# Two blocks on a diagonal in the products, the merge and the solve of a chunked recurrence; state scaled by pairs of chunks

## The chip, the cores and the metric

The kernel runs on one core of one Trainium2 chip. The metric is the device time of one execution in microseconds (us). A run of the kernel before took 594.81 us in the median of three (593.76 to 598.04). In the profile PE is TensorE (its matmuls; PEld its weight loads), DVE is VectorE, ACT is ScalarE, POOL is GpSimd, and SP is the engine that issues the DMAs.

## The reference

For 4 sequences of 768 steps with 8 heads of 40 channels a state matrix S (40 x 40 a head) is carried along, and the output of a step is read before the step changes it:

```
y[t]  = r[t] . S
Sa    = S a[t]
S     = S * w[t] - outer(Sa, b[t]) + outer(v[t], k[t])
```

w lies in 0.85 to 0.95, the other inputs are normal numbers times 0.05 or 0.1. The eight heads of a step form a row of 320 channels, and this goes through a layer norm without bias, a matmul to 1280 channels, ReLU, a matmul back to 320, and a residual sum (called the MoE layer below).

## The kernel before, in words

The 768 steps are cut into 24 chunks of 32 steps (C = 32, D = 40, B = 16). The 32 pairs of sequence and head are split into two halves of 16; one half's 40 channels stand on partitions 0 to 39, the other's on 64 to 103 (`ROWS`). Within a chunk the recurrence is solved in matrix form. The steps for a chunk, each a function of the program:

- `prep` loads w and a (`wa`), k and b (`bk`). Two scans on VectorE (L338, L342) make the running decay `gE` and its counterpart `qE`; GpSimd multiplies a by `qE` into `x2s` (L350) and k, b by `gE` (L356). TensorE then forms all products of a with k and b (L366): one matmul for each of 16 pairs-of-heads, with the 104 rows of both halves at once. So that the halves don't mix, GpSimd clears the rows that would meet the wrong half (L348). VectorE applies sign and mask (L369), and DMAs carry the result to a DRAM tile `d_l` and back into `x2s`.
- `invert` takes the 32 x 32 triangular matrices of a slab (two chunks, after two slabs of one) and inverts their two 16 x 16 diagonal blocks on GpSimd (L416, L420; on VectorE for the first two chunks), and puts them into `d_h` in DRAM.
- `merge` loads them back into `hv` and makes the full inverse by two groups of matmuls (L441, L452), one 32 x 32 tile of the array for each of four quarters (`QUADS`), with ScalarE's copies `qm` (L443) and `tt` (L454) between them.
- `loads` brings v, r and v transposed; `xk` gets k and b transposed. GpSimd clears the `z` rows of `x5s` (L483).
- `chain` is the recurrence itself: L498 multiplies the state, L508 solves with `tt`, L512 copies u, L523 forms the update, and VectorE adds the old state (L532) and scales with the decay of the next chunk (L533). The next chunk's L498 waits for it.
- `post` makes the output of the chunk: transposes of u and of the state (L551, L563), the products of v and u with r (L578, again 104 rows with both halves), their masking on VectorE (L584) and the output matmuls (L595).
- `norm` and `moe` are the layer behind it for every two chunks: dense matmuls L766 (first layer) and L750 (second layer), with ScalarE's ReLU copy `hh` (L769) and VectorE's rest `hl` (L771) between them.

Matmuls are on fp32 and each is executed as two matmul instructions and two weight loads, so 16 matmuls in the code are 32 in the trace. Products in the MoE layer are fp32r with hi and lo parts.

The order of the instructions is written out ahead of time by `Plan.order`. Every step is a task with an engine, an estimated time, a due time counted in chunks, the tiles it reads and writes, and the PSUM banks that it opens. The planner lays the tasks out engine by engine in simulated time: of what can start, the earliest due goes first. Of the eight PSUM banks four belong to group A (everything of the recurrence), two to the MoE's first layer and two to its second. The planner also limits how long small matmuls may run without dense ones between them, and counts matmul records against a price for fetching instructions. All DMAs are issued by SP in the planned order. On the chip each engine runs its tasks strictly in this order and waits on semaphores.

At the end the kernel looks over all w for values that it could not treat in this form, and would take a slow path, which these inputs do not need.

Of the kernel before, what the change touches and what calls it, by code (L numbers as in the profile page):

```python
# [11 lines left out]
F32 = mybir.dt.float32  # L12
# [4 lines left out]
ALU = mybir.AluOpType  # L17
# [165 lines left out]
def body(ctx, tc, ea, eb, vr, rd, vt, w1, w1x_in, w2, gl, fe, fd, out):  # L183
# [27 lines left out]
    start0, = ring(1, "start0", 16, 33)  # L211
# [11 lines left out]
    hv = ring(2, "hv", 8, 5 * B)  # L223
    qm, = ring(1, "qm", 8, C)
    tt = ring(2, "tt", 8, C)
# [22 lines left out]
    d_h = [dr.tile([32 * n, B, 3 * B], F32, name=f"d_h{s}") for s, (_, n) in enumerate(SLABS)]  # L248
# [10 lines left out]
    def dma(key, kb, rd, wr, to, of, parts=128, queue=2.0):  # L259
        P.add("SP", 0.35 + parts * 0.0006, lambda: sync.dma_start(out=to, in_=of), key, rd, wr, kb=kb, queue=queue)  # L260
# [3 lines left out]
    def consts():  # L264
# [27 lines left out]
        def f():  # L292
            V.memset(start0, 2.0 ** -33)
            V.memset(start0[:, :, 0:1], 1.0)
            V.memset(last, 0.0)
        op("DVE", 1.0, -95, (), ["start0", "last"], f)
        op("ACT", 0.3, -95, (), [("small", 0)], lambda: (A.memzero(small[0]["sd"]), A.sqrt(small[0]["sd"], small[0]["sd"])))
        for i in range(2):
            j = i + 1
            op("POOL", 0.8, -85 + i, (), two("hv", i, 4), lambda i=i: G.memset(hv[i], 0.0))  # L300

            def f(i=i):
                for q, qs in enumerate(QUADS):
                    up, lo = (ident[qs, 32 * q + B * x:32 * q + B * x + B].unsqueeze(1).broadcast_to([32, 8, B])
                              for x in range(2))
                    A.copy(out=hv[i][qs, :, 0:B], in_=lo)
                    A.copy(out=hv[i][qs, :, 4 * B:5 * B], in_=up)
                    if i == 0:
                        A.copy(out=qm[qs, :, 0:B], in_=lo)
            op("ACT", 2.6 if i == 0 else 1.8, -50 + i, ["ident"], two("hv", i, 4) + (["qm"] if i == 0 else []), f)  # L310
            op("POOL", 1.0, -40 + i, (), [("uT", i)] + two("vT", i), lambda i=i: G.memset(vu[i], 0.0))
            for t, x, us in ((x2, "x2", 1.4), (x5s, "x5s", 1.2), (xk, "xk", 1.4)):
                names = dict(
                    x2=two("S", i, 4) + two("v", i) + [("u", i)], x5s=two("r", i) + [("z", i)],
# [9 lines left out]
    def prep(c):  # L324
# [4 lines left out]
        W, K, A = two("wa", i), two("bk", k), two("x2a", x) + two("x2k", x, 4)  # L329
# [4 lines left out]
        for hf in (1, 0):  # L334
# [3 lines left out]
        op("DVE", 1.35, kp, W + ["start0"], [("g", i)], lambda: nc.vector.tensor_tensor_scan(  # L338
            out=flat(g[R]), data0=t[R, 0:n], data1=flat(start0[R]), initial=0.0, op0=ALU.mult, op1=ALU.max), lock=True)
        op("DVE", 0.29, kp, [("g", i)], ["last"], lambda: nc.vector.reciprocal(  # L340
            out=last[R, :, C:33], in_=g[R, :, C:33]))
        op("DVE", 1.4, kp, W + ["last"], [("q", i)] + ([("go",)] if c == 0 else []), lambda: nc.vector.tensor_tensor_scan(  # L342
            out=flat(q[R])[:, ::-1], data0=t[R, n:0:-1], data1=flat(last[R])[:, ::-1], initial=0.0,
            op0=ALU.mult, op1=ALU.max), lock=True)
        eng, e, us = ("DVE", nc.vector, 1.0) if c < EARLY else ("POOL", nc.gpsimd, 1.8)
        for hf, rs in enumerate(ROWS):
            if c >= XS:
                op("POOL", 0.6, kp - 0.3, (), [("x2k", x, 2 * hf), ("x2k", x, 2 * hf + 1)], lambda vs=slice(VROW[hf], VROW[hf] + C), hf=hf: nc.gpsimd.memset(  # L348
                    x2s[x][vs, hf, 0:512], 0.0))
# [3 lines left out]
            op("ACT", 0.25, kp + (1.0 if c < 2 else 0.0), [("g", i)], [("x2p", x, hf)], lambda hf=hf, rs=rs: nc.scalar.copy(  # L353
                out=x2s[x][rs, hf, 512:528], in_=g[rs, :, C:33].rearrange("p h o -> p (h o)")))
# [4 lines left out]
        b = Bank("A")  # L359

        def f(b=b):
            pg = bank[b.at].rearrange("p (f n t) -> p f n t", f=2, t=C)
            for h in range(8):
                for bb in range(2):
                    p = 8 * bb + h
                    mm(pg[64 * bb:64 * bb + 64, :, h], lhsT=tb[R, 64 * p:64 * p + 64], rhs=x2s[x][R, :, 32 * p:32 * p + 32],  # L366
                       start=True, stop=True)
        op("PE", 1.08, kp + 0.3, K + A, [b], f, opens=[b], room=[("gk", i)], recs=32.8)
        op("DVE", 0.72, kp + 0.3, [b, "sign"], [("gk", i)] + ([("first",)] if c == 1 else []), lambda b=b: nc.vector.tensor_tensor(  # L369
            out=gk[i].rearrange("p (n t) -> p n t", t=C), in0=bank[b.at].rearrange("p (n t) -> p n t", t=C),  # L370
            in1=sign.unsqueeze(1).broadcast_to([128, 16, C]), op=ALU.mult))
        for bb in range(2):
            m = 32 * j + 16 * bb
            dma(kp + 0.3, 140, [("gk", i)], [("d_l", s, 2 * j + bb)], d_l[s][m:m + 16].rearrange("m a t -> a m t"),
                gk[i][64 * bb + C:64 * bb + 64].rearrange("a (m t) -> a m t", t=C), 512)
        for hf in range(2):
            for bb in range(2):
                dma(kp + 0.4 + (1.0 if c < 2 else 0.0), 33, [("gk", i)], [("x2k", x, 2 * hf + bb)],
                    x2s[x][VROW[hf]:VROW[hf] + C, hf, 256 * bb:256 * bb + 256],
                    gk[i][64 * bb:64 * bb + C, 256 * hf:256 * hf + 256])  # L380
# [15 lines left out]
    def invert(s):  # L396
# [6 lines left out]
        eng, e, us = ("DVE", nc.vector, 0.54) if c0 < 2 else ("POOL", nc.gpsimd, 0.9)  # L403
# [3 lines left out]
        dma(k0, 262, L, Y, y[:, 0:1024], d_l[s].rearrange("m a t -> m (a t)"))  # L407
# [16 lines left out]
        dma(k0 + 0.4, 131, Y, [("d_h", s, 0)], d_h[s][:, :, B:3 * B], rows[:, 0:B])  # L424
# [544 lines left out]
```

## Time and profile before

| what | before |
|---|---|
| median of the runs | 594.81 us (593.76 to 598.04) |
| the profiled execution | 596.33 us, of which the span from first to last instruction is 594.6 |
| granted TensorE clock, mean | 0.961 |
| busy: TensorE, VectorE, ScalarE, GpSimd | 87%, 69%, 52%, 46% |
| matmul instructions | 14902, with as many weight loads |
| moved by DMA | 58.58 MB in 119670 packets |

The page gives busy time, the chain of work that ended last, and groups of instructions; a group's row has line, engine, operation, tiles out<-in, shapes, count, then busy time and mean duration, then idle time of the engine before them with what ended it. The rows of a stretch of time have TensorE's, its weight loads', VectorE's, ScalarE's and GpSimd's busy time with counts, the granted clock, the DMA share and the rate. Rows of the order of time have start, duration, engine, line, tiles and count.

### The profile page before, as it was taken

The numbers are of one execution on the slowest core, as the hardware profiler recorded it, in microseconds if no ns is written. First come the engines' busy times: TensorE is split into PE (matmuls) and PEld (weight loads), VectorE is DVE, ScalarE is ACT, GpSimd is POOL, SyncE is SP. The second block draws the span as 40 slices with busy tenths as digits, with TensorE's granted clock in tenths as the row PEclk, the third lists the DMA queues.
The fourth block names the chain that finished last, engine by engine and source line by source line (L and its number), as shares of the span: only waits on it lengthen the run. The fifth ranks groups of instructions, "written<-read, shape, count | busy, mean of one in ns | idle before, by whom it ended". The sixth has DMA issues, their size and how long they took to land.

```text
span 594.6 us, 33557 instructions
## 1 busy us (share of the span) xinstructions
PE 517.6 (87%) x14902; PEld 469.0 (79%) x14902; DVE 410.9 (69%) x907; ACT 311.2 (52%) x790; POOL 276.2 (46%) x510
## 2 busy tenths in 40 slices
PE   2527988799989899999899899899799899799996
PEld 2426766788879799888898798789799798688995
DVE  6699787787766667766676577686587667578622
ACT  8535768475465274373555365546456544555321
POOL 9425273374665572854824644674736706200000
PEclk9999779899989799998999899999999999899999
DMA  5465554425532435334243334434343344432000
GB/s 155 113 175 154 164 163 131 112 66 127 114 81 76 105 72 112 89 96 109 70 99 95 87 76 100 106 78 117 63 100 107 83 106 104 105 98 80 3 23 26
DMA packets 119670, 58.58 MB, mean 99 GB/s; under 512 B 100576, under 2 KB 106720, under 8 KB 119520
## 3 DMA queue, kind: packets, MB, share of 16 engines
q1 hardware_dynamic: 119520, 56.39, 38.6%
q8 instruction: 118, 1.93, 1.3%
q14 instruction: 32, 0.26, 0.1%
HBM read 44.56 MB, written 9.44 MB: 91 GB/s over the span
## 4 chain that ended last, share of the span: by engine, by line
PE 66%; POOL 8%; DVE 7%; issue 7%; ACT 5%; DMA 5%; SPq 1%; POOLq 0%; ACTq 0%; DVEq 0%
PE bank L750 17%; PE bank L766 16%; PE bank L366 4%; PE bank L578 4%; POOL ytmp L416 4%; POOL yv L420 4%; PE bank L595 2%; PE bank L498 2%; PE bank L508 2%; PE bank L441 2%; PE bank L452 2%; PE bank L563 2%; PE bank L473 2%; PE bank L523 2%; PE bank L551 2%
## 5 line engine op out<-in xcount | busy, mean ns | idle before, releaser
L750 PE MATMUL bank<-w,hh 128*128 128x320 f32 x480 | 119.9, 335 | 0.6 <-issue 0.6
L766 PE MATMUL bank<-xh,w 128*128 128x256 f32 x480 | 109.7, 290 | 4.4 <-issue 2.5
L769 ACT ACTIVATE hh<-bank 128x256 fp32r<-128x256 f32 x120 | 45.9, 384 | 116.4 <-PE bank L766 115.3
L771 DVE SCALAR_TENSOR_TENSOR hl<-bank,hh 128x256 fp32r<-128x256 f32 x120 | 49.9, 421 | 70.0 <-ACT hh L769 68.6
L766 PEld LDWEIGHTS bank<-xh,w 128*128 128x128 f32 x480 | 84.3, 193 | 4.4 <-issue 2.6
L750 PEld LDWEIGHTS bank<-w,hh 128*128 128x128 f32 x480 | 79.4, 195 | 7.6 <-issue 3.8
L356 POOL TENSOR_TENSOR bk<-bk,gE 104x1024 f32<-104x1024 f32 x22 | 48.9, 2222 | 65.7 <-issue 26.6
L750 PE MATMUL bank<-w,hl 128*128 128x320 f32 x240 | 76.2, 317 | 1.6 <-issue 1.6
L766 PE MATMUL bank<-xl,w 128*128 128x256 f32 x240 | 68.7, 286 | 0.2 <-issue 0.2
L350 POOL TENSOR_TENSOR x2s<-wa,qE 40x512 f32<-40x512 f32 x44 | 54.7, 1244 | 20.3 <-DVE qE L342 17.8
L420 POOL TENSOR_TENSOR yv<-yv,ytmp 64x28 f32<-64x28 f32 (+6 forms) x154 | 54.5, 354 | 12.1
L416 POOL TENSOR_TENSOR ytmp<-yv 64x28 f32<-64x28 f32 (+6 forms) x154 | 54.5, 354 | 11.4
L483 POOL MEMSET x5s<- 64x512 f32 x48 | 25.1, 522 | 71.6 <-PE bank L595 69.7
L532 DVE TENSOR_TENSOR bank<-bank,x 40x320 f32<-40x320 f32 x88 | 44.0, 500 | 11.2 <-PE bank L523 5.7
L478 ACT COPY xk<-bank 64x320 f32<-64x320 f32 x96 | 40.2, 419 | 21.7 <-PE bank L473 19.8
L584 DVE TENSOR_TENSOR x5s<-bank,mask 64x256 f32<-64x256 f32 x96 | 40.5, 422 | 15.4 <-PE bank L578 11.6
L766 PEld LDWEIGHTS bank<-xl,w 128*128 128x128 f32 x240 | 46.5, 194 | 3.1 <-issue 1.7
L750 PEld LDWEIGHTS bank<-w,hl 128*128 128x128 f32 x240 | 46.8, 195 | 1.4 <-issue 1.4
L512 ACT COPY x<-bank 32x320 f32<-32x320 f32 x96 | 40.1, 417 | 14.1 <-PE bank L508 12.8
L533 DVE TENSOR_TENSOR x<-bank,x2s 40x320 f32<-40x320 f32 x92 | 44.9, 489 | 3.1
L566 ACT COPY xk<-bank 40x320 f32<-40x320 f32 x96 | 40.2, 418 | 4.7 <-PE bank L563 3.0
L338 DVE TENSOR_TENSOR_SCAN gE<-wa,start 104x528 f32<-104x528 f32 x24 | 31.3, 1305 | 8.5 <-DMA wa<-in_ea_dram 4.8
(130 smaller groups left out, 1071.2 us busy)
## 6 DMA issues: line engine op xcount, KB each, us to landing
wa<-in_ea_dram SPq DMA_DIRECT2D x48, 162.7 KB
bk<-in_eb_dram SPq DMA_DIRECT2D x48, 160.0 KB
wa<-in_ea_dram SPq DMA_DIRECT2D x24, 165.0 KB
x<-in_vt_dram SPq DMA_DIRECT2D x48, 80.0 KB
x5s<-in_rd_dram SPq DMA_DIRECT2D x48, 80.0 KB
vu<-in_vr_dram SPq DMA_DIRECT2D x48, 80.0 KB
out_dram<-ot SPq DMA_DIRECT2D x24, 160.0 KB
r<-in_w_dram SPq DMA_DIRECT2D x10, 320.0 KB
```

Of the source, the lines that this page charges most:

```text
L350: op(eng, 0.75 * us, kp, W + [("q", i)], [("x2a", x, hf)], lambda hf=hf, rs=rs: e.tensor_tensor(out=x2s[x][rs, hf, 0:512].rearrange("p (h ...
L356: op(eng, 1.25 * us, kp, [("g", i)], K, lambda: e.tensor_tensor(out=kb, in0=kb, in1=g[R, :, 0:C].unsqueeze(2).broadcast_to([104, 16, 2, C] ...
L416: e.tensor_tensor(out=tv, in0=yb[:, :, j + 1:, j:j + 1].broadcast_to(S), in1=yb[:, :, j:j + 1, 0:j].broadcast_to(S), op=ALU.mult)
L420: e.tensor_tensor(out=v, in0=v, in1=tv, op=ALU.add)
L478: op("ACT", 0.45, c - 1.2 + 0.1 * bb, [bs[hf]], [X[hf]], lambda b=bs[hf], zs=zs, hf=hf, bb=bb: nc.scalar.copy(out=xk[i][zs, hf, 8 * bb:8 * ...
L532: nc.vector.tensor_tensor(out=p, in0=p, in1=x2[i][rs, hf, ps], op=ALU.add)
L533: nc.vector.tensor_tensor(out=x2[o][rs, hf, ps], in0=p, in1=x2s[xo][rs, hf, 512 + 8 * bb:520 + 8 * bb].unsqueeze(2).broadcast_to([D, 8, D] ...
L584: op("DVE", 0.46, k + 0.5, [b, "mask"], [("z", i)], lambda b=b, zs=zs, ps=ps, hf=hf, bb=bb: nc.vector.tensor_tensor(out=x5s[i][zs, hf, 8 * ...
L750: mm(bank_of(po[u])[:, 0:CH], lhsT=l[:, us], rhs=ws[f"w2_{f // 2}"][:, f % 2, x], start=f == 0 and n == 0, stop=f == 9 and n == 2)
L766: mm(ph, lhsT=l, rhs=r, start=n == 0, stop=n == 7)
L769: yield "ACT", 0.39, [phs[f]], [("hh", f % 2)], lambda f=f: nc.scalar.activation(out=hht[f % 2], in_=bank_of(phs[f])[:, 0:256], func=AF.Re ...
L771: yield "DVE", 0.46, [phs[f], ("hh", f % 2)], [("hl", f % 2)], lambda f=f: nc.vector.scalar_tensor_tensor(out=hlt[f % 2], in0=bank_of(phs[ ...
```

## The change: what it does

- **Products.** The matmuls of a with k and b (L366) and of r with v and u (L578) are done for each half by itself, on its 40 rows: 32 matmuls in the code in place of 16, each 32 wide in place of 64. The two halves go to two banks, and together with the two output halves (partitions 0 to 63 and 64 to 127) they make four tiles of the array. Nothing has to be cleared for this, so GpSimd's fills L348 and L483 are left out. VectorE takes each bank by itself (two operations in place of L369).
- **Merge and solve.** Two quarters are put on the diagonal of one 64 x 64 block. `hv` has nine blocks of 16 columns, `qm` four, `tt` 64 columns; the matmuls of L441, L452 and L508 become half as many, on 64 rows. ScalarE's copy into `tt` becomes four, one for each quarter, since each has its own columns. `d_h` is stored by rows, and the loads into `hv` differ between even and odd quarters (for the even ones three pieces of 16 columns, apart).
- **v with room for u.** The host lays v transposed with 32 zeros behind each 32 values. The load fills the whole tile `vu` in long runs, the half for u too.
- **State by pairs.** The decay is counted over two chunks. `qE` is scanned first, from a start table with 1 at the end for even chunks, and from the even chunk's last column for odd ones; `gE` follows from its reciprocal. The state is then only added after an even chunk, and added and scaled after an odd one. After chunk 0 ScalarE copies it.
- **The planner's costs** are changed along with it: the task times of the new groups, a time for each DMA's issue, and sizes of some DMAs.

```diff
+        h = c % 2
+        if h:
+            op("DVE", 0.15, kp, [("q", 0)], [("start", 1)], lambda: nc.vector.tensor_copy(
+                out=start[1][R, :, C:33], in_=qE[0][R, :, 0:1]))
...
         for hf, rs in enumerate(ROWS):
-            if c >= XS:
-                op("POOL", 0.6, kp - 0.3, (), [("x2k", x, 2 * hf), ("x2k", x, 2 * hf + 1)], ... memset(
-                    x2s[x][vs, hf, 0:512], 0.0))
...
-                    mm(pg[64 * bb:64 * bb + 64, :, h], lhsT=tb[R, 64 * p:64 * p + 64], rhs=x2s[x][R, :, 32 * p:32 * p + 32],
-                       start=True, stop=True)
+                    for hf, rs in enumerate(ROWS):
+                        p = 8 * bb + h
+                        mm(bank[bs[hf].at][64 * bb:64 * bb + 64, C * h:C * h + C], lhsT=tb[rs, 64 * p:64 * p + 64],
+                           rhs=x2s[x][rs, hf, 32 * p:32 * p + 32], start=True, stop=True)
...
-                for qs in QUADS:
-                    mm(po[qs, h], lhsT=qm[qs, h], rhs=right[qs, h], start=True, stop=True)
-        op("ACT", 0.4, km, [b], [("tt", i)], lambda b=b: nc.scalar.copy(
-            out=tt[i], in_=bank[b.at][:, 0:8 * C].rearrange("p (h t) -> p h t", h=8)))
+                for ps in halves:
+                    mm(po[ps, h], lhsT=qm[ps, h], rhs=blocks(hv[i], 4)[ps, h], start=True, stop=True)
+        for q, qs in enumerate(QUADS):
+            op("ACT", 0.39, km, [b], [("tt", i, q)], lambda b=b, qs=qs, q=q: nc.scalar.copy(
+                out=tt[i][qs, :, C * (q % 2):C * (q % 2) + C],
+                in_=bank[b.at][qs, 0:8 * C].rearrange("p (h t) -> p h t", h=8)))
...
-            dma(c - 0.6, 82, (), [("vT", i, hf)], vu[i][rs, :, 0], vr[c, hf])
+            dma(c - 0.6, 110, (), [("vT", i, hf), ("uT", i)], vu[i][rs], vr[c, hf])
...
-            op("POOL", 0.6, c - 0.7, (), [("z", i)], lambda zs=zs, hf=hf: nc.gpsimd.memset(x5s[i][zs, hf], 0.0))
...
-                for qs in QUADS:
-                    mm(bank[b.at][qs, h * D:h * D + D], lhsT=tt[i][qs, h], rhs=hn[i][qs, h], start=True, stop=True)
+                for ps in (slice(0, 64), slice(64, 128)):
+                    mm(bank[b.at][ps, h * D:h * D + D], lhsT=tt[i][ps, h], rhs=hn[i][ps, h], start=True, stop=True)
...
+                        if c == 0:
+                            nc.scalar.copy(out=to, in_=p)
+                        elif c % 2 == 0:
+                            nc.vector.tensor_tensor(out=to, in0=p, in1=old, op=ALU.add)
+                        else:
+                            nc.vector.tensor_tensor(out=p, in0=p, in1=old, op=ALU.add)
+                            nc.vector.tensor_tensor(out=to, in0=p, in1=x2s[x][rs, hf, ...], op=ALU.mult)
...
-                    mm(pz[64 * bb:64 * bb + 64, :, h], lhsT=vu[i][R, p].rearrange("p x t -> p (x t)"), rhs=x5s[i][R, :, p],
-                       start=True, stop=True)
+                    for hf, rs in enumerate(ROWS):
+                        p = 8 * bb + h
+                        mm(bank[bs[hf].at][64 * bb:64 * bb + 64, C * h:C * h + C], lhsT=vu[i][rs, p].rearrange("p x t -> p (x t)"),
+                           rhs=x5s[i][rs, hf, p], start=True, stop=True)
```

165 lines of the change are left out of this document (84 added, 81 removed).

## The prediction

> **What bounds the kernel now.** I read the page first, for the engines and the chain of waits, then the table by stages, then the groups, then the order of instructions on TensorE.
>
> ```profile
> span 594.6 us, 33557 instructions
> ...
> PE 517.6 (87%) x14902; PEld 469.0 (79%) x14902; DVE 410.9 (69%) x907; ACT 311.2 (52%) x790; POOL 276.2 (46%) x510
> ...
> PE 66%; POOL 8%; DVE 7%; issue 7%; ACT 5%; DMA 5%; SPq 1%; POOLq 0%; ACTq 0%; DVEq 0%
> ```
>
> ```profile
> core 0: us, PE busy (x) PEld busy (x) DVE busy (x) ACT busy (x) POOL busy (x), PEclk, DMA share, GB/s
> 0.00:120.00 120.00, 77.97 (x2067) 64.87 (x2071) 94.45 (x205) 73.57 (x178) 59.33 (x106) 0.91 0.55 144
> 120.00:560.00 440.00, 410.89 (x12638) 375.82 (x12627) 306.67 (x677) 231.36 (x596) 216.87 (x405) 0.97 0.39 92
> ```
>
> Two thirds of the chain is TensorE. The stages tell where. In the first 120 us TensorE is busy for 78 us and VectorE for 94: start-up and weights set the pace. From 120 to 560 us TensorE is busy 410.9 of 440 us, ScalarE only 231 and GpSimd 217. So I treat the stretch after 120 us as bound by TensorE and price the change by what TensorE's groups of matmuls cost there. A busy time is no price, since matmuls overlap; the price of a group is the time from its start to the start of the group behind it, where the two stand without a gap. These are pieces of TensorE's order of time (start, duration, line, tiles, count):
>
> ```profile
> 265.96 0.72 PE L441 MATMUL bank<-hv 32*32 32x16 f32 x64
> 266.61 1.15 PE L578 MATMUL bank<-x5s,vu 104*64 104x64 f32 x32
> 267.70 0.75 PE L452 MATMUL bank<-hv,qm 32*32 32x32 f32 x64
> 268.38 1.15 PE L366 MATMUL bank<-x2s,bk 104*64 104x64 f32 x32
> 269.46 0.56 PE L750 MATMUL bank<-w,hh 128*128 128x320 f32 x2
> ...
> 296.23 0.48 PE L473 MATMUL bank<-ident,bk 40*64 40x40 f32 x16
> 296.64 1.15 PE L366 MATMUL bank<-x2s,bk 104*64 104x64 f32 x32
> 297.72 0.79 PE L508 MATMUL bank<-hn,tt 32*32 32x40 f32 x64
> 298.44 0.55 PE L733 MATMUL bank<-ident,xn 128*128 128x128 f32 x3
> ...
> 301.12 0.83 PE L523 MATMUL bank<-x,xk 64*40 64x40 f32 x64
> 301.88 0.64 PE L551 MATMUL bank<-ident,x 32*40 32x32 f32 x32
> 302.45 0.41 PE L750 MATMUL bank<-w,hh 128*128 128x320 f32 x1
> ```
>
> Start to start: the two merge groups L441 0.65 and L452 0.68 us; the products L578 1.09 and L366 1.08; the solve L508 0.72; L523 0.76; L551 0.57; L473 0.41. The two products are the dearest, with half as many matmuls as their neighbours. The reason to be read from the rows is what passes through a tile of the array, not the number of matmuls. L366 is 32 matmuls of 64 columns on two tiles (the two column halves): 16 rounds. L452 is 64 of 32 columns on four tiles, also 16 rounds, and costs 0.40 less. L551, 32 matmuls of 32 columns on two tiles, again 16 rounds, costs 0.57, not half of L452.
>
> How many of these groups lie in the bound stretch, from the groups after 120 us:
>
> ```profile
> L578 PE MATMUL bank<-x5s,vu 104*64 104x64 f32 x672 | 26.1, 234 | 0.6 <-ACT vu L554 0.3 <-issue 0.3
> L366 PE MATMUL bank<-x2s,bk 104*64 104x64 f32 x576 | 21.7, 230 | 2.4 <-issue 1.6 <-POOL bk L356 0.7
> ...
> L508 PE MATMUL bank<-hn,tt 32*32 32x40 f32 x1344 | 16.6, 199 | 0.5 <-ACT hn L501 0.5
> L452 PE MATMUL bank<-hv,qm 32*32 32x32 f32 x1280 | 15.8, 196 | 3.0 <-issue 2.1 <-ACT vu L554 0.9
> L441 PE MATMUL bank<-hv 32*32 32x16 f32 x1280 | 15.2, 181 | 3.7 <-issue 3.5
> ```
>
> That is 21 groups of L578 (672/32), 18 of L366, 21 of L508 and 20 each of L452 and L441.
>
> **The change, part by part.**
>
> *Products (L366, L578).* Each becomes 64 matmuls of 32 columns on 40 rows, on four tiles: two row halves by two column halves. Moving width and count are those of L452 (0.68); the placement on two row halves by two column halves is that of L523 (0.76, with 40 columns). I take 0.69, since the width is L452's; the bounds are L441's 0.65 and L523's 0.76. Saved 1.08 - 0.69 = 0.39, times 39 groups: 15.2 us (12.5 to 16.8).
>
> *Merge.* Two groups of 64 on four small tiles become two groups of 32 on two 64-row tiles, 32 columns wide. L551 has count, width and two tiles: 0.57. I take 0.58 each; the bounds are 0.57 and L508's 0.72. Saved 0.65 + 0.68 - 1.16 = 0.17, times 20: 3.4 us (from 3.8 down to a loss of 2.2).
>
> *Solve.* 32 matmuls on two tiles in place of 64 on four, still 40 wide. L551's 0.57 for 32 columns makes 0.71 for 40, against 0.72: halving the matmuls saves nothing, 0.2 us over 21 groups.
>
> Sum on TensorE after 120 us: 15.2 + 3.4 + 0.2 = 18.8 us.
>
> *Instruction stream.* Matmuls fall by 32 a chunk (two products +32 each, merge -64, solve -32), 768 of 14902, 5%. At most that share of the chain's 7% "issue" goes with them, 2 us; I count none.
>
> *ScalarE.* One copy of the merged matrix (L454) becomes four, one for each 32 rows. L512 copies 32 rows of a bank.
>
> ```profile
> L512 ACT COPY x<-bank 32x320 f32<-32x320 f32 x96 | 40.1, 417 | 14.1 <-PE bank L508 12.8
> ...
> L454 ACT COPY tt<-bank 128x256 f32<-128x256 f32 x24 | 8.9, 371 | 15.4 <-PE bank L452 15.2
> ```
>
> Four at no more than 0.417 against 0.371 is 1.3 us more a chunk, 26 us over 20 chunks, on an engine busy for 231 of 440. I cost it at nothing: the idle 209 us hide it. Without that cover it is the ACT rival below.
>
> *VectorE.* The state is scaled only after odd chunks, so half of L533 goes.
>
> ```profile
> L532 DVE TENSOR_TENSOR bank<-bank,x 40x320 f32<-40x320 f32 x80 | 40.0, 501 | 10.7 <-PE bank L523 5.2 <-ACT hh L769 3.6
> L533 DVE TENSOR_TENSOR x<-bank,x2s 40x320 f32<-40x320 f32 x80 | 39.1, 489 | 2.8
> L584 DVE TENSOR_TENSOR x5s<-bank,mask 64x256 f32<-64x256 f32 x84 | 35.5, 422 | 12.9 <-PE bank L578 10.4
> ```
>
> 40 of the 80 at 0.489 is 19.6 us less, and an even chunk's state is ready four operations (2 us) earlier. Against it the signed product is taken in two halves, at most two of L584's 0.42 where one was. With VectorE at 307 of 440 this moves the end by nothing, in my sum. In the first 120 us, where VectorE leads, chunks 0 and 2 lose four operations each (-3.9 us), the second start table adds one fill, priced as one such operation, and ScalarE's three extra copies stand in the first chunk's chain (+1.3): bounds -3.9 and +2, taken as 0.
>
> The two scans change places, and an odd chunk's scan starts from the even chunk's last column, through a copy of 16 columns; both stand in VectorE's order one after the other already, so the wait adds nothing. ScalarE's two small copies of the decay are made in odd chunks alone.
>
> *GpSimd.* All clearing of tiles before the products goes, four fills a chunk:
>
> ```profile
> L483 POOL MEMSET x5s<- 64x512 f32 x40 | 20.9, 523 | 71.3 <-PE bank L595 69.7
> L348 POOL MEMSET x2s<- 32x512 f32 x33 | 17.1, 520 | 23.0 <-PE bank L498 16.9 <-issue 4.4 <-POOL bk L356 0.5
> ```
>
> 38 us of work and 94 us of standing still ahead of it, with the scaling of k, b and the inversion queued behind. It was off the bound, so 0; the bound on the gain is in the second case below.
>
> *DMA and SP.* v is loaded with zeros beside it: twice the bytes, but 40 long runs instead of 640 short ones, so the issue on SP is shorter and not longer. It now also has to land before ScalarE writes u into the same tile; behind that copy stand ScalarE's ReLU copies. It can be issued as early as before, so 0. The even quarters of the merge's load go in pieces of a third; no row has that, from 0 to some tenths of SP time. The two-halves layout lets the copies of the first half leave before the second is done.
>
> **Sum.** The profiled execution took 596.3 us, span 594.6 and 1.7 around it; 596.3 - 18.8 = 577.5. The median of the runs is 1.5 below the profiled one, so the forecast is 594.8 - 18.8 = 576. Its own range, by the bounds above, the prologue's -3.9 to +2 and 2 us of issue: 568 to 587.
>
> **The cases.** A measurement here tells about 1%, 6 us, from no change.
>
> *TensorE's groups shrink as priced: 576, chance 0.58.* For it speak the unbroken rows above.
>
> *More than that: 562, chance 0.17.* TensorE stands idle for 29 of the 440 us, which belong to the others' lateness. If lighter VectorE, GpSimd and SP halve it, another 14 us go.
>
> *The products' gain is given back: 591, chance 0.12.* Each product now opens two of the four banks of its group where one did. If TensorE waits 0.39 at each for a second bank, only 3.6 of the 18.8 remain. The plan is made anew and can place them otherwise, hence the small chance.
>
> *ACT becomes late: 602, chance 0.08.* The four copies stand in ScalarE's queue ahead of the ReLU copies (L769) that the second layer's matmuls await. If each chunk's 1.3 us shows, 26 us over 20 chunks, the end is 594.8 - 18.8 + 26. It decides once the ReLU copy has less than 1.3 us to spare. Against it, ScalarE waits for TensorE before that copy, not the other way round:
>
> ```profile
> ACT hh L769 <- PE bank L766: 115.3, 88, 4.9
> ```
>
> *Weights bind: 613, chance 0.05.* L473 loads 64 columns of weights on two row halves for each of 16 matmuls in 0.41, 26 ns each. If that is the weights' price, a product of 64 such loads costs 1.64, 0.56 more than now: 39 times that is +22, less 3.6. Against it, L366 has 32 such loads in 1.08, and L473's price is also explained by its 40 moving columns in eight rounds. The Trainium skill, "TensorE: Matmul & The Clock Gate", section "LDWEIGHTS (loading the stationary operand)", gives columns/1.2 ns for a load, 53 ns for 64 columns, and Part 3 lets loads overlap matmuls only where the row group differs. By that rule I estimate 1.7 us for a product after the change, two row groups sharing 64 loads, about the price of this rival; but it asks 1.7 also of L366 with one row group, and the trace has 1.08, so the trace does not agree.
>
> Faster by over 1%: 0.58 + 0.17 = 0.75; within 1%: 0.12; slower: 0.13. The range 560 to 598 leaves out the two slow cases and the far end of the second.
>
> **What would show it.** After the change, start to start in unbroken rows: the products at 0.65 to 0.76 with 64 matmuls, the merge groups near 0.58, the solve at 0.71 in spite of its 32. GpSimd's fills of these tiles gone, about 20 us less of VectorE, 25 us more of ScalarE. TensorE's busy share in the middle should stay near 93%: if it falls and the groups did shrink, a wait took the gain, and its releaser (ACT's copies or a bank's reader) names the rival. If the products stay at 1.08, the reading by moving columns is wrong.

## The result, and the profile after

The changed kernel took 627.94 us in the median of four runs (623.41 to 631.58), the one before 595.55 us (593.76 to 598.04) beside it: a ratio of 1.054, with a 95% interval of 1.045 to 1.062. The change made the kernel slower by 5%; 576 us had been forecast, between 560 and 598. The profiled execution took 625.96 us. Its page has these lines for busy time, the granted clock in 40 slices, and the chain of waits:

```profile
span 624.2 us, 32083 instructions
...
PE 559.8 (90%) x14134; PEld 510.3 (82%) x14134; DVE 398.4 (64%) x896; ACT 336.4 (54%) x842; POOL 231.7 (37%) x424
...
PEclk9999557699579769999999999999999899999998
...
PE 77%; DMA 5%; DVE 5%; POOL 4%; issue 3%; ACT 3%; SPq 2%; ACTq 0%; POOLq 0%; DVEq 0%
```

All that was to become lighter did: VectorE 411 to 398 us, GpSimd 276 to 232, matmuls 14902 to 14134, "issue" on the chain (time in which an engine waits for nothing that the profile shows) from 7% to 3%. ScalarE rose by 25 us, as forecast. TensorE rose by 42 us of busy time, and its share of the chain from 66% to 77%. The table by stages, with the columns of the one shown of before:

```profile
0.00:120.00 120.00, 75.86 (x1593) 63.17 (x1595) 93.05 (x193) 67.84 (x160) 52.33 (x82) 0.80 0.55 142
120.00:560.00 440.00, 425.92 (x11510) 392.22 (x11508) 273.78 (x629) 244.11 (x619) 179.41 (x343) 0.94 0.40 96
```

From 120 to 560 us TensorE stands idle for 14 us; before it was 29. So no new wait took a gain. TensorE works more and gets through less: 11510 matmuls in this stretch against 12638, 9% fewer, where the whole kernel has 5% fewer. Two things are behind it. The first stands in TensorE's order of time (start, duration, line, tiles, count), in rows without a gap:

```profile
409.64 1.12 PE L523 MATMUL bank<-hn,tt 64*64 64x40 f32 x32
410.69 0.39 PE L785 MATMUL bank<-xh,w 128*128 128x256 f32 x1
...
422.47 1.14 PE L597 MATMUL bank<-x5s,vu 40*64 40x32 f32 x64
423.54 0.47 PE L583 MATMUL bank<-ident,x 40*40 40x40 f32 x16
...
425.95 1.12 PE L458 MATMUL bank<-hv 64*64 64x32 f32 x32
427.01 0.87 PE L614 MATMUL bank<-xk,x5s 128*32 128x40 f32 x64
427.81 1.12 PE L468 MATMUL bank<-hv,qm 64*64 64x32 f32 x32
428.86 0.47 PE L492 MATMUL bank<-ident,bk 40*64 40x40 f32 x16
...
431.28 1.14 PE L375 MATMUL bank<-x2s,bk 40*64 40x32 f32 x64
432.35 0.48 PE L492 MATMUL bank<-ident,bk 40*64 40x40 f32 x16
```

Start to start, the solve (L523) is at 1.05 us, the product of r (L597) and that of a (L375) at 1.07, the merge groups (L458, L468) at 1.06 and 1.05. The products did not become cheaper than their 1.08 and 1.09 by more than 0.02; the merge went from 0.65 + 0.68 to 2.11 and the solve from 0.72 to 1.05.

The second is the row PEclk: between about 60 and 240 us five of its slices stand at five or six, where the row of before never falls below seven:

```profile
PEclk9999779899989799998999899999999999899999
```

The stages where the time was lost are the same. VectorE's last operation on the MoE output of the fourth and of the seventh pair of chunks, and of the last one, starts before at

```profile
281.36 0.49 DVE L778 SCALAR_TENSOR_TENSOR ot<-bank,xt 128x320 f32<-128x320 f32 x1 [1.33 <-PE bank L750]
...
414.43 0.89 DVE L778 SCALAR_TENSOR_TENSOR ot<-bank,xt 128x320 f32<-128x320 f32 x2
...
588.20 0.93 DVE L778 SCALAR_TENSOR_TENSOR ot<-bank,xt 128x320 f32<-128x320 f32 x2 [0.51 <-PE bank L750]
```

and after at

```profile
315.97 0.89 DVE L797 SCALAR_TENSOR_TENSOR ot<-bank,xt 128x320 f32<-128x320 f32 x2
...
440.38 0.93 DVE L797 SCALAR_TENSOR_TENSOR ot<-bank,xt 128x320 f32<-128x320 f32 x2 [0.84 <-PE bank L769]
...
617.58 0.93 DVE L797 SCALAR_TENSOR_TENSOR ot<-bank,xt 128x320 f32<-128x320 f32 x2 [0.51 <-PE bank L769]
```

The changed kernel is 35 us late after four pairs, 26 after seven and 29 at the end: all of the loss arises in the first half, and none of it in the steady part. That doesn't fit groups that are dearer in every chunk, taken alone.

### The profile page after: what moved, and what is told of

Its sections match the earlier page's. It is cut to its first block, busy times and chain, and to the rows that moved or that the text cites. A ratio compares the mean times of both kernels' runs of the same rounds, so it can differ in the third digit from the quotient of the medians.

```text
span 624.2 us, 32083 instructions
## 1 busy us (share of the span) xinstructions
PE 559.8 (90%) x14134; PEld 510.3 (82%) x14134; DVE 398.4 (64%) x896; ACT 336.4 (54%) x842; POOL 231.7 (37%) x424
## 3 DMA queue, kind: packets, MB, share of 16 engines
q8 instruction: 112, 1.84, 1.3%
## 4 chain that ended last, share of the span: by engine, by line
PE 77%; DMA 5%; DVE 5%; POOL 4%; issue 3%; ACT 3%; SPq 2%; ACTq 0%; POOLq 0%; DVEq 0%
PE bank L769 18%; PE bank L785 18%; PE bank L375 4%; PE bank L523 4%; PE bank L468 4%; PE bank L597 4%; PE bank L458 4%; PE bank L614 3%; PE bank L538 3%; PE bank L583 3%; PE bank L492 3%; PE bank L513 2%; PE bank L571 2%; SPq L263 2%; PE bank L400 2%
## 5 line engine op out<-in xcount | busy, mean ns | idle before, releaser
L769 PE MATMUL bank<-w,hh 128*128 128x320 f32 x480 | 118.6, 332 | 1.2 <-issue 1.1
L358 POOL TENSOR_TENSOR x2s<-wa,qE 40x512 f32<-40x512 f32 x44 | 56.9, 1293 | 161.3 <-PE bank L513 76.9
L785 PE MATMUL bank<-xh,w 128*128 128x256 f32 x480 | 113.0, 298 | 0.0
L785 PEld LDWEIGHTS bank<-xh,w 128*128 128x128 f32 x480 | 86.6, 199 | 1.6
L432 POOL TENSOR_TENSOR yv<-yv,ytmp 64x28 f32<-64x28 f32 (+6 forms) x154 | 52.8, 343 | 12.1
L428 POOL TENSOR_TENSOR ytmp<-yv 64x28 f32<-64x28 f32 (+6 forms) x154 | 51.6, 335 | 11.3
L497 ACT COPY xk<-bank 64x320 f32<-64x320 f32 x96 | 40.1, 418 | 28.0 <-PE bank L492 26.3
L471 ACT COPY tt<-bank 32x256 f32<-32x256 f32 x96 | 34.9, 363 | 21.2 <-PE bank L468 20.1
L458 PE MATMUL bank<-hv 64*64 64x32 f32 x768 | 30.3, 229 | 15.7 <-DMA hv<-d_h 13.8
L375 PE MATMUL bank<-x2s,bk 40*64 40x32 f32 x1536 | 34.9, 241 | 10.3 <-ACT bank L657 3.3
L375 PEld LDWEIGHTS bank<-x2s,bk 40*64 40x64 f32 x1536 | 31.8, 159 | 13.5 <-ACT bank L657 3.5
```

The lines of the kernel that those rows point to most:

```text
L358: op(eng, 0.75 * us, kp, W + [("q", i)], [("x2a", x, hf)], lambda hf=hf, rs=rs: e.tensor_tensor(out=x2s[x][rs, hf, 0:512].rearrange("p (h ...
L375: mm(bank[bs[hf].at][64 * bb:64 * bb + 64, C * h:C * h + C], lhsT=tb[rs, 64 * p:64 * p + 64], rhs=x2s[x][rs, hf, 32 * p:32 * p + 32], star ...
L428: e.tensor_tensor(out=tv, in0=yb[:, :, j + 1:, j:j + 1].broadcast_to(S), in1=yb[:, :, j:j + 1, 0:j].broadcast_to(S), op=ALU.mult)
L432: e.tensor_tensor(out=v, in0=v, in1=tv, op=ALU.add)
L458: mm(po[ps, h], lhsT=hv[i][ps, h, 0:4 * B], rhs=blocks(hv[i], 5)[ps, h], start=True, stop=True)
L497: op("ACT", 0.45, c - 1.2 + 0.1 * bb, [bs[hf]], [X[hf]], lambda b=bs[hf], zs=zs, hf=hf, bb=bb: nc.scalar.copy(out=xk[i][zs, hf, 8 * bb:8 * ...
```

## The experiments

Each kernel is given with its median and its ratio to the kernel before on the same chip; the kernels ran on several chips, so that of two kernels the ratios compare better than the medians. The planner lays the order out anew for each, so a per cent between two kernels can come from the order alone. Unless said otherwise an edit is made to the changed kernel.

### Products or merge: one part undone at a time

The first run undoes the merge and the solve (four tiles of 32 x 32, as before) and keeps the split products:

```diff
-                for ps in halves:
-                    mm(po[ps, h], lhsT=hv[i][ps, h, 0:4 * B], rhs=blocks(hv[i], 5)[ps, h], start=True, stop=True)
-        op("PE", 0.56, km, two("hv", i, 4), [b], f, opens=[b], room=["qm"], recs=32.5)
+                for qs in QUADS:
+                    mm(po[qs, h], lhsT=hv[i][qs, h, 0:2 * B], rhs=hv[i][qs, h, 3 * B:4 * B], start=True, stop=True)
+        op("PE", 0.66, km, two("hv", i, 4), [b], f, opens=[b], room=["qm"], recs=64.5)
...
```

> The changed kernel with merge and solve undone (64 matmuls on four 32 x 32 tiles each, one copy into tt), all else changed. Theory W (loads of 64 weight columns set the price of a group): the two merge groups go from 0.95 and 1.04 back to 0.66 and 0.68 us and the solve from 1.06 to 0.72, 1.0 us a chunk, about 20 us: 608. Theory C (the half clock in the first 240 us took the time, and the longer groups are what brings it): half-clock time falls from 108 us to about 50 as before and the time to 580 or less. Theory P (the new products are to blame): no change, 628.

The second undoes the products (104 rows, with GpSimd's fills) and keeps merge and solve joined:

```diff
-                    for hf, rs in enumerate(ROWS):
-                        p = 8 * bb + h
-                        mm(bank[bs[hf].at][64 * bb:64 * bb + 64, C * h:C * h + C], lhsT=tb[rs, 64 * p:64 * p + 64],
-                           rhs=x2s[x][rs, hf, 32 * p:32 * p + 32], start=True, stop=True)
-        op("PE", 0.7, kp + 0.3, K + two("x2a", x), bs, f, opens=bs, room=two("gk", i), recs=64.8)
+                    p = 8 * bb + h
+                    mm(pg[64 * bb:64 * bb + 64, :, h], lhsT=tb[R, 64 * p:64 * p + 64], rhs=x2s[x][R, :, 32 * p:32 * p + 32],
+                       start=True, stop=True)
+        op("PE", 1.08, kp + 0.3, K + A, [b], f, opens=[b], room=two("gk", i), recs=32.8)
...
```

> The changed kernel with the products undone (32 matmuls over all 104 rows, GpSimd's fills are back), merge and solve joined. Theory W: a product costs 1.07 either way, so the time stays within 1% of 628, slightly up for the fills. Theory C with the products' fewer rows as what lowers the clock: half-clock time falls and the time goes to about 600. Theory P: back to 600 or less.

With the merge undone it took 648.74 us (1.090, interval 1.082 to 1.097); with the products undone 601.42 (1.010, 1.001 to 1.019). Undoing the part whose groups had become dearer made the kernel slower still, and undoing the part whose groups cost what they had cost won 26 us. So the prices of the groups are not all of it. The first kernel has 16438 matmuls, the second 12598.

### Both undone; and the planner told what the groups cost

Both undone, by the two edits above together (the solve's shown here), leaves the state by pairs, the room for u, the order of `d_h` and the planner's new DMA costs:

```diff
-                for ps in (slice(0, 64), slice(64, 128)):
-                    mm(bank[b.at][ps, h * D:h * D + D], lhsT=tt[i][ps, h], rhs=hn[i][ps, h], start=True, stop=True)
+                for qs in QUADS:
+                    mm(bank[b.at][qs, h * D:h * D + D], lhsT=tt[i][qs, h], rhs=hn[i][qs, h], start=True, stop=True)
...
```

> Products, merge and solve all as before; what stays of the change is the state by pairs, v with room for u, the layout of d_h and the planner's DMA prices. Theory W: 628 - 20 for merge and solve, and the shorter work of VectorE and SP helps: 575 to 590, under the kernel before. Theory C with the pairs' new start-up as its cause: still above 600, with the half clock in the first 240 us.

587.67 us (0.988, interval 0.980 to 0.996). What is left of the change is no loss, and perhaps a gain of 1%.

The other run keeps the changed kernel's work and corrects only the task times by which the planner orders it:

```diff
-        op("PE", 0.7, kp + 0.3, K + two("x2a", x), bs, f, opens=bs, room=two("gk", i), recs=64.8)
+        op("PE", 1.07, kp + 0.3, K + two("x2a", x), bs, f, opens=bs, room=two("gk", i), recs=64.8)
...
-        op("PE", 0.56, km, two("hv", i, 4), [b], f, opens=[b], room=["qm"], recs=32.5)
+        op("PE", 1.04, km, two("hv", i, 4), [b], f, opens=[b], room=["qm"], recs=32.5)
...
-        op("PE", 0.72, k, two("tt", i, 4) + [("hn", i)], [b], f, opens=[b], room=[("u", i)], recs=32)
+        op("PE", 1.06, k, two("tt", i, 4) + [("hn", i)], [b], f, opens=[b], room=[("u", i)], recs=32)
...
```

> The changed kernel with the planner's task times set to what the trace after shows (merge 1.04 and 1.05 where 0.56 stood, solve 1.06 for 0.72, products 1.07 for 0.70); the work is the same. Theory L (a plan made from wrong prices lays small matmuls too long in a row, the clock falls and TensorE waits): 10 to 30 us less, half-clock time down. Theory W alone: within 1% of 628.

608.06 us (1.023, interval 1.015 to 1.032): with the same instructions in another order 20 of the 32 us are gone. The granted clock of this kernel by slices, and its stages:

```profile
PEclk9999999689999999989999999999999999999998
```

```profile
0.00:120.00 120.00, 78.65 (x1584) 66.09 (x1586) 93.18 (x193) 69.23 (x163) 51.70 (x83) 0.95 0.55 143
120.00:280.00 160.00, 153.85 (x4283) 141.27 (x4279) 99.87 (x229) 93.51 (x236) 73.40 (x138) 0.98 0.40 98
280.00:560.00 280.00, 273.94 (x7747) 253.47 (x7747) 188.78 (x427) 162.86 (x413) 105.05 (x204) 1.00 0.41 102
```

The clock is 0.95 up to 120 us where it was 0.80 in the changed kernel. The time at half clock falls from 107.7 us, as the trace's clock records add up, to 26.3 in this execution. But it is the fastest of the four (604.18) and the only one at a mean clock of 0.98: the others took 606 to 612 us at 0.94, which makes some 70 to 75 us at half clock, as the records hold only full and half. So 45 us less at half clock went with 2 to 8 us in this kernel. The 20 us came with the order made from right task times; how much of them is the clock's, and why this order is granted more of it, the runs don't tell.

### What sets the price of a group

A kernel of its own issues groups of the same shapes between blocks of dense matmuls; it isn't the computation. Each shape is a list of tiles (first row, rows, first column), with W weight columns and N moving ones:

```diff
+            for h in range(8):
+                for t in range(2):
+                    mm(**args(DIAG, 64, 32, h, t))
+            dense(16)
...
```

> Not the computation: only fp32 matmul groups of eight rounds in the code (16 executed), each behind 16 dense matmuls, with weight columns, moving columns and tiles varied one at a time. Theory W (a round lasts as long as the loads of the weights' columns of one tile, whatever the tiles beside it and the moving columns): with 64 columns every group takes 0.88 to 0.93 us from its first to its last start, for 16, 32 and 64 moving columns, on two diagonal tiles, on two column halves or on four tiles; with 32 columns 0.55 to 0.60, also with 64 moving; with 40 columns about 0.62. Theory M (the prediction's, moving columns set it): with 64 weight columns 0.45 for 16 and 32 moving columns and 0.93 for 64; with 32 weight columns and 64 moving 0.93.

Rows of its order of time; behind the tiles stand rows*columns of the weights, then rows x moving columns:

```profile
30.42 0.73 PE L50 MATMUL bank<-x,w 32*32 32x16 f32 x64
38.18 0.75 PE L54 MATMUL bank<-x,w 32*32 32x32 f32 x64
45.96 1.11 PE L58 MATMUL bank<-x,w 64*64 64x16 f32 x32
54.11 1.12 PE L62 MATMUL bank<-x,w 64*64 64x32 f32 x32
62.26 1.15 PE L66 MATMUL bank<-x,w 64*64 64x64 f32 x32
70.44 0.69 PE L70 MATMUL bank<-x,w 64*32 64x32 f32 x32
78.17 1.08 PE L74 MATMUL bank<-x,w 64*32 64x64 f32 x32
86.29 1.14 PE L78 MATMUL bank<-x,w 40*64 40x32 f32 x64
94.46 1.10 PE L82 MATMUL bank<-x,w 40*32 40x64 f32 x64
102.59 0.83 PE L86 MATMUL bank<-x,w 40*40 40x40 f32 x64
110.45 1.12 PE L90 MATMUL bank<-x,w 104*64 104x32 f32 x32
```

Every group here is 16 rounds through each of its tiles. With 64 weight columns it lasts 1.11 to 1.15 us, whether 16, 32 or 64 columns move (L58, L62, L66). With 32 weight columns and 64 moving ones it is 1.08 and 1.10 as well (L74, L82). With 32 of each it is 0.69 and 0.75 (L70, L54), with 40 of each 0.83 (L86). So in these products the larger of the two numbers sets a round; neither "weights alone" nor "moving columns alone" holds. Two tiles or four makes no difference (L62 and L78). Joining two 32 x 32 blocks to one of 64 x 64 doubles the weight columns, and that is the whole price; splitting the products halved the moving columns from 64 to 32 and left 64 weight columns, and so the price stayed. The transposes against the identity are an exception: in the changed kernel's rows above L492, with 64 weight columns, and L583, with 40, both last 0.47 us. They are also one instruction each in the trace, and not two, as these products are.

### The start table's copy on ScalarE

In the changed kernel VectorE's copy of 16 columns into the start table stands long:

```profile
L347 DVE COPY start<-qE 104x16 f32<-104x16 f32 x12 | 10.3, 862 | 0.0
```

The first of the twelve begins at 11.8 us and lasts 4.38 us, while GpSimd runs its fills of `x`, `x5s`, `xk`, `tt` and `x2s` without a gap from 10.1 to 16 us; the shortest copy takes 0.12. The Trainium skill, "SBUF — State Buffer", section "SBUF: two separate sides", says that GpSimd and VectorE, in some of its modes, share a port pair under an exclusive lock, held for a whole instruction; a wait of this length beside those fills agrees with that, but no run here took the fills away. The run moves the copy to ScalarE in the kernel with both parts undone:

```diff
-            op("DVE", 0.15, kp, [("q", 0)], [("start", 1)], lambda: nc.vector.tensor_copy(
+            op("ACT", 0.25, kp, [("q", 0)], [("start", 1)], lambda: nc.scalar.copy(
```

> As e4 (products, merge and solve as before, the rest of the change kept), and the copy of 16 columns into the second start table is done by ScalarE in place of VectorE. Theory K (on VectorE this copy stands still behind GpSimd's fills and products, 2.4 us for the first one and 7 us in all): the first chunks come 2 to 4 us earlier, and the time falls from 588 to 583 to 586. If the copy was covered: 588.

590.84 us (582.28 to 595.36; 0.992, interval 0.983 to 1.002) against 587.67 (0.988): no gain is seen. On ScalarE the first copy starts at 7.7 us and takes 0.22, so the length on VectorE was real; the end did not come earlier by as much as the spread of the runs could show, and the 2 to 4 us expected are less than that spread.

### The right prices for each part alone

The joined merge and solve with the old products, as in the second run, and the planner told 1.04, 1.05 and 1.06 for the three groups:

```diff
-        op("PE", 0.56, km, two("hv", i, 4), [b], f, opens=[b], room=["qm"], recs=32.5)
+        op("PE", 1.04, km, two("hv", i, 4), [b], f, opens=[b], room=["qm"], recs=32.5)
...
```

> As e2 (merge and solve joined, products as before), with the planner told 1.04, 1.05 and 1.06 us for the three groups. Theory W: 20 us more of TensorE than e4 over the bound stretch, less what fewer matmuls (12598) save in instruction transfers: 590 to 600. Theory L: the right prices alone take 10 us off e2's 601.

The split products alone, as in the first run, told 1.07:

```diff
-        op("PE", 0.7, kp + 0.3, K + two("x2a", x), bs, f, opens=bs, room=two("gk", i), recs=64.8)
+        op("PE", 1.07, kp + 0.3, K + two("x2a", x), bs, f, opens=bs, room=two("gk", i), recs=64.8)
...
```

> As e1 (new products, merge and solve as before), with the planner told 1.07 us for a product in place of 0.70. The matmuls are the most of all kernels, 16438. Theory L (wrong prices): from 649 back to 590 or so. Theory F (instructions: 128 matmuls with their loads come in one transfer of 16 KB, never under 3.3 us apart in the traces, and 687 matmuls a chunk make 5.4 of them, 18 us or more): it stays above 605.

The joined merge and solve now take 585.85 us (0.981, interval 0.973 to 0.989), 15.6 less than with the wrong times, and the lowest median of the study, 2% below the kernel before (against both undone, 587.67, the intervals overlap). The split products take 646.79 (1.086, 1.077 to 1.095) after 648.74 (1.090): their right price changes nothing that the runs can tell. The stretch from 120 to 560 us, of the joined one

```profile
120.00:560.00 440.00, 434.93 (x10957) 403.12 (x10957) 301.09 (x662) 259.27 (x657) 217.98 (x410) 1.00 0.41 99
```

and of the split one

```profile
120.00:560.00 440.00, 399.95 (x12875) 364.32 (x12875) 256.26 (x591) 210.37 (x534) 177.07 (x337) 0.90 0.36 92
```

With the joined merge TensorE is idle for 5 of 440 us at full clock. With the split products it is idle for 40, at 0.90, although the array's time by the groups' prices is the same as in the kernel with both undone. Per chunk the split products are two groups of 64 matmuls where the old ones are two of 32. From "both undone" to "split" the 1536 matmuls more go with 59 us more; from "joined" to the changed kernel with right times (608.06), again the split products alone, with 22.

### Is it the number of matmuls?

Two groups are issued twice in each chunk, the second time with the same result into the same bank: the output products (64 short matmuls), or the product of r with v and u in its old form (32 long ones). Each is put into two kernels, the one with both parts undone and the one with merge and solve joined at right times.

```diff
-            for h in range(8):
-                for y in range(4):
+            for h, y in [(h, y) for _ in range(2) for h in range(8) for y in range(4)]:
...
-            for h in range(8):
-                for bb in range(2):
+            for h, bb in [(h, bb) for _ in range(2) for h in range(8) for bb in range(2)]:
```

> Base: old products, old merge, old solve, pairs kept (587.67 us, 14902 matmuls). Here the products with r's scores (64 small matmuls, 0.72 to 0.76 us start to start) are issued twice in each of the 24 chunks, the second time with the same result into the same bank; the planner is told 1.5 us for both. Array theory (a group costs its own start to start, whatever it counts): +24 x 0.74 = +18 us, about 606. Count theory (each matmul beyond what the stream delivers costs its share of the stream; 59 us for the 1536 matmuls that split products add to this base, 38 ns each): +1536 x 38 ns = +59 us, about 647.

> Same base (587.67 us). Here the later products (32 matmuls, 1.07 us start to start) are issued twice in each chunk; the planner is told 2.16 us. Array theory: +24 x 1.07 = +26 us, about 613, more than for the small ones. Count theory: +768 x 38 ns = +29 us, about 617, half of what the small ones cost. The order of the two runs tells the theories apart.

> Base: old products, joined merge and solve with measured prices (585.85 us, 12598 matmuls). The 64 small matmuls twice in each chunk: 14134 matmuls, the same number as the changed kernel. Array theory: +24 x 0.74 = +18 us, about 604. Count theory with room in the stream (this base counts 2304 fewer): by the 22 us that split products add to this base, 14 ns a matmul, +22 us, about 608. Nearly the same, so this run tells only whether 14134 matmuls of another make take what the changed kernel with measured prices takes (608.06).

> Same base (585.85 us). The later products twice in each chunk: 13366 matmuls. Array theory: +24 x 1.07 = +26 us, about 612. Count theory: +768 x 14 ns = +11 us, about 597, where the array is not the limit; if the array is the limit here, the run lies by the array theory and above the run with the small ones.

TensorE's order of time first tells what the repeats cost the array. With the short ones repeated:

```profile
400.68 1.38 PE L609 MATMUL bank<-xk,x5s 128*32 128x40 f32 x128
401.99 0.47 PE L483 MATMUL bank<-ident,bk 40*64 40x40 f32 x16
...
414.75 1.15 PE L592 MATMUL bank<-x5s,vu 104*64 104x64 f32 x32
415.83 0.44 PE L461 MATMUL bank<-hv,qm 32*32 32x32 f32 x29
```

and with the long ones:

```profile
405.73 2.08 PE L592 MATMUL bank<-x5s,vu 104*64 104x64 f32 x64
407.75 0.75 PE L461 MATMUL bank<-hv,qm 32*32 32x32 f32 x64
...
410.44 0.80 PE L609 MATMUL bank<-xk,x5s 128*32 128x40 f32 x64
411.17 0.48 PE L483 MATMUL bank<-ident,bk 40*64 40x40 f32 x16
```

The short repeat adds 1.31 - 0.73 = 0.58 us, 13.9 over 24 chunks; the long one 2.02 - 1.08 = 0.94, 22.6. By the array the long ones should be the dearer. The end of the kernel says the opposite:

| repeated | in | matmuls more | array, us | median, us | ratio (interval) | more than its base, us |
|---|---|---|---|---|---|---|
| 64 short | both undone | 1536 | 13.9 | 625.04 | 1.062 (1.048 to 1.076) | 37 |
| 32 long | both undone | 768 | 22.6 | 613.19 | 1.041 (1.029 to 1.054) | 26 |
| 64 short | joined | 1536 | 13.9 | 615.86 | 1.043 (1.021 to 1.066) | 30 |
| 32 long | joined | 768 | 22.6 | 600.84 | 1.021 (1.008 to 1.034) | 15 |

In both pairs the short ones lie above the long ones in every run (622.2 to 627.8 against 609.9 to 614.4; 613.9 to 623.9 against 598.3 to 602.7). The last column goes by medians from different chips; by the ratios each repeat costs 6 to 9 us more (44, 32, 37 and 24), in the same order. So the long ones cost about their array time, between two thirds of it and 1.4 times. The short ones cost two to three times theirs: 24 and 20 ns for each matmul by the medians (37/1536 and 30/1536), 29 and 24 by the ratios, where the array takes 9. So short matmuls have a price by number, of some 20 to 29 ns, that a group in an unbroken row doesn't show. It has one weakness: the repeat also keeps the chunk's output and its bank 0.58 us longer, and the order is planned anew.

The traces name the wait. TensorE's instructions come by a DMA queue of their own in transfers of 16 KB: 130 of them for the 16438 matmuls of the split products, 118 for 14902, 100 for 12598. In none of these kernels do two of them start less than 3.2 us apart. In the stretch from 120 to 560 us TensorE waits by "issue" for 30 us in 27 places with the split products, 25 us in 23 places with the short repeats in the same base, and 10 us in 12 places in that base itself. Each of these 62 waits ends 1.2 to 1.7 us after the end of such a transfer, and from one to the next TensorE executes a multiple of 127 to 128 matmuls: it stands at the end of a transfer's worth of instructions. In the long repeats it is 12 us in that base and 1 us in the joined one, against 9 for the short ones there and 2 without a repeat. From these figures an estimate: 128 matmuls in 3.2 us are 25 ns each. A group that uses one matmul in 17 ns (1.07/64, a split product) runs ahead of the transfers, one that uses it in 34 (1.08/32, the old product) does not.

The size expected from the split products, 38 ns each, was too high for the repeats. Their 59 us divide in the profiled executions, whose spans differ by 55 (640.9 against 585.6): TensorE is idle for 20 us more (91.6 against 71.6) and busy for 35 us more, although the groups cost the same at full clock. What is left for the 35 is the lower clock, 0.89 in the mean against 0.96, at which a group lasts longer (shown at the end); why it is granted less is open.

## Why the prediction was wrong

**What bounds the kernel** was right: TensorE, after 120 us, and still so after the change (66% of the chain before, 77% after). What it left out is that TensorE also waits for its own instructions.

**Products, 0.69 for 1.08: wrong.** They stayed at 1.07. The step that failed is the pricing of a round by the moving columns, "since the width is L452's". A round goes by the larger of moving and weight columns, and the split product kept 64 weight columns. Most rows quoted could not tell: L366 had 64 of both, L452 32 of both. L441 is the row that would have spoken: with 32 weight columns and 16 moving ones it costs 0.65, hardly less than L452's 0.68, and by moving columns it should have been far cheaper; the prediction used it as a bound. L473, 64 weight columns and 40 moving ones, speaks the other way, but it is a transpose. Expected were -15.2 us; the groups gave 39 times 0.01 to 0.02.

**Merge, 0.58 for each group: wrong by the same step.** 2.11 for the two in place of 1.16: over 20 groups +15.6 us, not -3.4. The bound of a loss of 2.2 was too narrow, because every row that it came from has 32 or 40 weight columns. The 0.57 came, besides, from L551, a transpose: the small kernel's matmuls of 32 columns on two tiles last 0.69, and L551 lasts 0.64.

**Solve, 0.71: wrong again.** 1.05, so over 21 groups +6.9 and not -0.2. The sum of these terms is +22 us where -18.8 stood.

**"Weights bind", 613, chance 0.05,** was right that 64 weight columns bind, from a row that doesn't show it: L473 is a transpose, and inside it a round lasts 36 ns. It had been put aside since L366 has 32 loads in 1.08. But that is 16 rounds on each of two tiles with the loads of the tiles beside one another, and no contradiction: inside a group, from one matmul of a tile to its next, a round of 64 columns lasts 58 to 59 ns in the records of both kernels. The figure of the Trainium skill, "TensorE: Matmul & The Clock Gate", section "LDWEIGHTS (loading the stationary operand)", columns/1.2 ns, 53 ns for 64 columns, agrees with a round of the products and not with one of L473; what doesn't agree is Part 3's rule that loads overlap only where the row group differs, by which the two tiles of L90 in the small kernel, in one row group, should cost more than those of L62, in two: both take 1.12. The rival's time, 613, was above the kernel at right times (608) and below the changed one (628); its mechanism, 64 loads one after another, was not the right one either.

**Instruction stream "I count none": wrong, and in both directions.** Merge and solve have 96 matmuls fewer in a chunk; the products have 64 more. The joined groups cost 22 us more on the array by the terms above, and yet joined with right times (585.85) and both undone (587.67) take the same. The 2304 matmuls fewer are the likely reason: from 120 to 560 us TensorE is idle for 5 us in the joined kernel and for 21 in the other, 2 and 10 of them by "issue", at a clock of 1.00 and 0.98; how much of the 22 us each of these paid back is argued, not shown. The split products pay for 1536 more without a gain on the array: +22 us onto the joined kernel, +59 onto the one with both undone.

**The planner's costs** were described and then given no term. Told 0.56, 0.72 and 0.70 for groups of 1.05 and 1.07, the planner made an order that took 20 us more, nearly as much as the split products, and had the half clock for 108 us in the profiled execution.

**"More than that"**: its premise held (idle TensorE fell from 29 to 14 us, as lighter VectorE, GpSimd and fewer matmuls would make it, but also longer groups), and it was outweighed. **Banks** and **ScalarE late** did not occur: from 120 to 560 us TensorE waited less than 2 us in all just before the products, and ScalarE grew by 25 us, as forecast, while its share of the chain fell from 5% to 3%.

**GpSimd, VectorE:** GpSimd lost 44 us of work for the 38 forecast, VectorE 12.5 for 19.6, since the copies that were priced at nothing take 10.3. "The wait adds nothing" was wrong for the copy; for the time nothing speaks against it, as moving the copy away gave no gain that could be seen.

The whole in steps, each a run, in one order of several (the split products cost 22 us in this one and 59 where the merge is not joined): before 595.6; pairs, room for u and the rest 587.7; merge and solve joined at right times 585.9; products split 608.1; wrong times 627.9.

## What to carry to other kernels

Price a group of small matmuls (transposes apart) by the larger of its weight columns and its moving columns, and test a reading of rows against one row in which the two differ before 39 groups are multiplied by it. Then count the matmuls as well, at some 25 ns each in this kernel, where they are shorter than that on the array: joining blocks need not lose although the array takes longer, and splitting can cost although it takes no longer. Where an order is planned from task times, the change is not done until the new times are measured and put back; here that alone decided between 601 and 586 us for the joined merge.

## What the runs showed of the hardware

The granted clock fell to half in a stretch in which TensorE had hardly a gap. The table of two neighbouring stretches of the changed kernel:

```profile
157.00:181.00 24.00, 23.27 (x494) 21.64 (x494) 12.52 (x28) 9.48 (x26) 4.71 (x3) 0.51 0.39 101
181.00:205.00 24.00, 23.66 (x617) 21.91 (x611) 14.94 (x32) 13.92 (x34) 15.09 (x33) 1.00 0.35 80
```

TensorE is busy for 23.3 and 23.7 of 24 us, at a clock of 0.51 and 1.00. Busy time stretches with the slower clock, so the engine looks equally loaded in both. In the first a product costs 1.7 times as much:

```profile
162.12 1.93 PE L597 MATMUL bank<-x5s,vu 40*64 40x32 f32 x64
163.85 1.91 PE L375 MATMUL bank<-x2s,bk 40*64 40x32 f32 x64
165.69 1.29 PE L513 MATMUL bank<-x,x2s 96*32 96x40 f32 x64
166.77 1.29 PE L614 MATMUL bank<-xk,x5s 128*32 128x40 f32 x64
167.99 0.74 PE L492 MATMUL bank<-ident,bk 40*64 40x40 f32 x16
```

Start to start, L597 and L375 are at 1.73 and 1.84 us for 1.07, L614 at 1.22 for 0.80. The Trainium skill, "TensorE: Matmul & The Clock Gate", section "What's actually happening", has the gate follow how busy TensorE was in windows of some 3.4 us, and fall back after an idle one; the trace's clock records hold two levels, full and half, in pieces of 3.4 us and multiples of it, but here the clock was halved without an idle window, as far as the modelled ends of matmuls can tell. Why one order is granted the full clock and the other not, these runs leave open.
